# A deeper ring for raw weights in the first block, and four w_out parts split ahead

## The chip, the cores and the metric

The kernel runs on one core of a Trainium2 chip. The metric is the device time of one launch, in microseconds (us). Engines are named as in the profile: PE is TensorE's matrix multiply and PEld its weight load, DVE is VectorE, ACT is ScalarE, POOL is GpSimd, SP is SyncE, which here only issues transfers (SPq is its queue). L12 means line 12 of the kernel before.

## The reference

Attention in a window of 64 positions, then two layers of two matrix products each.

```python
def _attn_ref(q, k, v):            # (4, 8, 576, 64) each
    scores = scale * np.matmul(q, k.transpose(0, 1, 3, 2))
    ...
    mask = (rel >= 0) & (rel < 64)
    ...                            # softmax over the masked scores
    return np.matmul(attn, v)
def reference(...):
    x = attention, as (2304, 512)
    x = softplus(x @ w_in) @ w_out           # w_in (512, 2048), w_out (2048, 512)
    return piecewise_square(x @ w2_in) @ w2_out
```

softplus(h) is max(h, 0) + log1p(exp(-|h|)); the second layer's function is h for h >= 1, 0 for h <= -1 and (h + 1)^2 / 4 between.

## The kernel before, in words

**Split numbers.** Most products are taken with operands split into a high and a low part, both of the type fp32r: three matmuls (high by high, high by low, low by high) replace one of full f32.

**Weights.** Each layer's d_ff of 2048 is cut into 16 parts f. The host hands over the inputs viewed as 64-bit integers; a "raw" tile [128, 512, 2] of 512 KB holds one half of a part. Half j = 2f is the w_in part of f, half 2f + 1 its w_out part, for j below 32; the second layer's w_in has halves 32 to 47 and its w_out 48 to 63. `load_w` (L138) issues the next raw load from SP, into a ring of four tiles (`NRAW`, tag "raw"). The same ring also gives the tiles "o", in which `finish` (L428) collects a block's result before its store to x2d, and they come in the order of the program. Decoding a half is one ScalarE pass (`begin_half`, L162) and three VectorE passes (`end_half`, L167 to L169); when the opening is over, `end_half` of a first-layer half also calls `load_w`. `high` (L178, ScalarE) and `low` (L185, VectorE) make the two split parts. For w_in they go into the large tile `area`; for w_out (part 1) into tiles of the tags "wh1" (16 tiles of 2 KB per partition) and "wl1" (17).

**The first layer** goes over five blocks of tokens, 512, 256, 512, 512 and 512. For each block and part f, `g1` (L400) does 12 matmuls of x by w_in into one of two banks "h", `softplus` (L418, or L423 to L425 in the split form) makes g from it, and two steps later `g2` (L411) adds g by w_out into four banks "y". Block 0 differs: its w_out part is the decoded f32 tile `wo`, not split, and its g is one f32 tile, so that `g2` is a plain f32 product:

```python
if len(g) == 1:
    ops = [(wo[f][:, c], g[0])]
else:
    a, b = wh[0, f, 1], wl[0, f, 1]
    ops = [(a[:, c], g[0]), (a[:, c], g[1]), (b[:, c], g[0])]
```

From block 1 on everything is split. The loop over steps splits the parts `wo` into "wh1" and "wl1" tiles in block 1 (`osplit`), just ahead of their use. At the last step of block 1 it calls `load_w(3)` for the first three halves of the second layer; the steps of blocks 2 and 3 decode that layer's w_in (`decode_win`), and store it to DRAM (wd), and the last block splits its w_out (`split_wout`) into tiles of the same tags "wh1" and "wl1".

**Attention** for the next block runs between these steps: scores (L282), copies and mask (L304, L306, L310), maximum (L314, L315), exponentials (L319), normalising (L324 to L326), transposes (L336), masks (L346), values (L363), and x as high and low (L368, L371). Its q, k and v loads are issued from SP.

**The order of the work.** The opening, up to the first parts of block 0, is written out by hand in the list START: a letter for each operation (W a raw load, R and B the two stages of a decode, H and L high and low, G, U and Z the three stages of a part, S to Y the attention, K and J its loads). After it, and on engines that the list leaves idle, the framework's planner takes the ready instruction that comes first in the program, by its own estimate of times. So an instruction of a later block may run early: its place in the code is no more than its rank. Each engine then runs its list in this order, and waits where an input is late. Tiles of one tag are handed out in the order of the program.

Of the kernel before, what the change touches and what calls it, by code (L numbers as in the profile page):

```python
# [9 lines left out]
F32 = mybir.dt.float32  # L10
F32R = mybir.dt.float32r
I32 = mybir.dt.int32  # L12
# [5 lines left out]
NT, DM, DFF = B * S, H * D, 2048  # L18
P = 128
# [4 lines left out]
NF = DFF // P  # L24
# [15 lines left out]
HALF = 256  # L40
BEHIND = 8
NRAW = 4
NHALF = 4
NFIRST = 6


# [5 lines left out]
W5 A1 P0 B2 X0 E11 E10 H2 Y0 B3 N1 S2 C20 J1 C21 D20 W6 D21 T1 A2 E21 V10 V11 E20 P1 J2 N2 T2 L0 V21 V20 W7 P2  # L52
K3 J3 X1 R4 Y1 R5 X2 B4 H4 Y2 G00 L2 L4 U00 B5 S3 R6 W8 C30 C31 D30 D31 G20 R7 G10 J4 U20 Z20 A3 B6 B7 R8 E30
Z00 W9 E31 N3 T3 R9 U10 K4 Z10 H6 W10 L6 V30 R10 V31 G30 W11 B8 U30 P3 X3 W12 Z30 H8 R11 Y3 B9 B10 G11 U11 G31
H10 G01 L8 B11 U31 L10 W13 G21 Z11 U01 U21 G52 G42 Z01 U52 Z21 U42 Z31 Z52 Z42 J5
""".split()


# [1 line left out]
def tile_window_attention_two_ffn(  # L60
# [13 lines left out]
    wpool = ctx.enter_context(tc.tile_pool(name="weights", bufs=NF))  # L74
    spool = ctx.enter_context(tc.tile_pool(name="stage", bufs=3))
# [45 lines left out]
    def cut(at, n):  # L121
        return area[:, at:at + n]
# [9 lines left out]
    wh, wl, wo = {}, {}, {}  # L132
# [5 lines left out]
    def load_w(n=1, e=nc.sync):  # L138

        for _ in range(n):  # L140
            j = wnext[0]
            if j < (2 if wlimit[0] else 4) * NF:
                raw = spool.tile([P, DM, 2], I32, tag="raw", name="raw", bufs=NRAW)
                f, part = divmod(j, 2) if j < 2 * NF else (j % NF, j // NF - 2)
                e.dma_start(raw.rearrange("p c w -> p (c w)"),
                            (w1, w2)[j // (2 * NF)][f, :, 2 * DM * part:2 * DM * (part + 1)])
                raws[j] = raw
                wnext[0] += 1
# [3 lines left out]

    def begin_half(j):

        if j < 2 * NF and j % 2:
            t = wpool.tile([P, DM], F32, tag="wl1", name="wo", bufs=NF + 1)
            wo[j // 2] = t
            t = t.bitcast(I32)
        else:
            t = tpool.tile([P, DM], I32, tag="o", name="bits")  # L160
        decoded[j] = t
        A.activation(t.bitcast(F32), raws[j][:, :, 1].bitcast(F32), AF.Copy, scale=2.0 ** -112)  # L162

    def end_half(j):
        t, raw = decoded[j], raws.pop(j)
        lo, hi = raw[:, :, 0], raw[:, :, 1]
        V.tensor_scalar(t, t, 3, 1, op0=ALU.logical_shift_left, op1=ALU.bitwise_or)  # L167
        V.scalar_tensor_tensor(t, hi, -2 ** 31, t, op0=ALU.bitwise_and, op1=ALU.bitwise_or)  # L168
        V.scalar_tensor_tensor(t, lo, 29, t, op0=ALU.logical_shift_right, op1=ALU.bitwise_or)  # L169
        if not opening[0] and j < 2 * NF:  # L170
            load_w()

    def high(key, t, part):
        if part:
            wh[key + (part,)] = wpool.tile([P, DM], F32R, tag="wh1", name="wh1")
        else:
            wh[key + (part,)] = cut(2 * DM * key[1], DM)
        A.copy(wh[key + (part,)], t)  # L178

    def low(key, t, part):  # L180
        if part:
            wl[key + (part,)] = wpool.tile([P, DM], F32R, tag="wl1", name="wl1", bufs=NF + 1)
        else:
            wl[key + (part,)] = cut(2 * DM * key[1] + DM, DM)
        V.tensor_tensor(wl[key + (part,)], t, wh[key + (part,)].bitcast(F32), op=ALU.subtract)  # L185

    def split_w(f):
        for part in range(2):
            j = 2 * f + part
            begin_half(j)  # L190
            end_half(j)
            t = decoded.pop(j)
            if not part:
                high((0, f), t.bitcast(F32), 0)
                low((0, f), t.bitcast(F32), 0)

    kept = []

    def keep_w():

        while kept:
            f = kept.pop()
            nc.sync.dma_start(wd[f // 2][:, DM * (f % 2):DM * (f % 2 + 1)], decoded.pop(2 * NF + f).bitcast(F32))
            load_w()

    def decode_win(f):
        keep_w()
        begin_half(2 * NF + f)
        end_half(2 * NF + f)
        kept.append(f)  # L210
# [165 lines left out]
    def new_x():  # L376
        return [xpool.tile([P, KC, 512], F32R, tag=t, name=t) for t in ("xh", "xl")]

    def attn_items(block, xh, xl):

        t0, n = block
        items = []
        for i in range(n // P):
            a = attention(t0 // P + i, "a", "a", "a", xh, xl, i * P)
            items += [[(a["S"],), (a["C"], 0), (a["C"], 1), (a["D"], 0), (a["D"], 1), (a["A"],)],
                      [(a["E"], 0), (a["E"], 1), (a["N"],)],
                      [(a["T"],), (a["V"], 0), (a["V"], 1)],
                      [(a["P"],), (a["X"],), (a["Y"],)]]
        return items
# [24 lines left out]
    def softplus(h, n, split):  # L414

        if not split:
            g = gpool.tile([P, 512], F32, tag="gl", name="g")[:, :n]
            A.activation(g, h, AF.Softplus)  # L418
            return (g,)
        e = tpool.tile([P, 512], F32, tag="e", name="e")[:, :n]  # L420
        gh = gpool.tile([P, 512], F32R, tag="gh", name="gh")[:, :n]
        gl = gpool.tile([P, 512], F32R, tag="gl", name="gl")[:, :n]
        A.activation(gh, h, AF.Softplus)  # L423
        A.activation(e, h, AF.Softplus)  # L424
        V.tensor_tensor(gl, e, gh.bitcast(F32), op=ALU.subtract)  # L425
        return gh, gl

    def finish(block, y):  # L428
        t0, n = block
        per = 1024 // n  # L430
        for m0 in range(0, len(y), per):
            o = spool.tile([P, 1024], F32, tag="raw", name="o", bufs=NRAW)
            for m in range(m0, m0 + per):
# [52 lines left out]
    def load_x2(blk):  # L486

        for name, kc, hf in (("B11", 0, 0), ("B12", 0, 1), ("B22", 2, 1), ("B21", 2, 0)):
            if blk:
                st = spool.tile([P, 2, NW], F32, tag="raw", name="xs", bufs=NRAW)  # L490
            else:
# [12 lines left out]
    def split_x(name, slot):  # L504
        h, l = piece(slot)
        A.copy(h, xt[name])
        V.tensor_tensor(l, xt[name], h.bitcast(F32), op=ALU.subtract)
# [34 lines left out]
    def second(blk, p, g, t):  # L542
# [9 lines left out]
        if p == NQ - 1:  # L552
            o = spool.tile([P, DM], F32, tag="raw", name="o", bufs=NRAW)
            r = slice(WIDE * blk + t * P, WIDE * blk + (t + 1) * P)
# [9 lines left out]
    def emit(item, i, g):  # L564

        for step in item:
            step[0](*step[1:])
        d = g + i // 4 * 2
        if i % 4 < 2:
            load_qk(d + i % 4 + 2)  # L570
        elif i % 4 == 3:
            load_v(d + 4)
            load_v(d + 5)
# [5 lines left out]
    for i, (_, n) in enumerate(BLOCKS):  # L579
        kf = 512 // n  # L580
        steps += [(i, f, kf, 0, n) for f in range(0 if i else NFIRST, NF, kf)]
    pend = []
    wsplit = [0]
    osplit = [0]
# [57 lines left out]
    for i, f, kf, c0, n in steps:  # L642
        if i < last:
            nb = BLOCKS[i + 1][1] // P * 4
            if i + 1 not in xs:
                xs[i + 1] = new_x()
                queue = attn_items(BLOCKS[i + 1], *xs[i + 1])
            d = nb - len(queue)
            while d < ((f + kf) * nb // NF if i else (f + kf - BEHIND) * nb // (NF - BEHIND)):
                emit(queue.pop(0), d, BLOCKS[i + 1][0] // CB)  # L650
                d += 1

        if i == 0:
            while wsplit[0] < min(f + kf + AHEAD, NF):
                split_w(wsplit[0])
                wsplit[0] += 1
        if i == 1:
            while osplit[0] < min(f + kf, NF):
                t = wo.pop(osplit[0])
                high((0, osplit[0]), t, 1)  # L660
                low((0, osplit[0]), t, 1)
                osplit[0] += 1
            if f + kf == NF:
                wlimit[0] = False
                load_w(3)
        if 2 <= i <= 3 and f % 2:
            decode_win(NF // 2 * (i - 2) + f // 2)

        if i == last:
            if f == 0:  # L670
                keep_w()
                begin_second()
                load_x2(0)
                load_pair(0)
            if f == 3:
                combine(0)
                load_pair(1)
            if f >= 4:
                split_wout(f - 4)
            if f % 2 and f > 1:  # L680
                name = FIRST[f // 2 - 1]
                if name[0] == "T":
                    term(name)
                split_x(name, slots[name])
        h = pt("h")[:, :kf * n]
        for j in range(kf):
            g1(f + j, c0, n, *xs[i], h[:, j * n:(j + 1) * n])
        if len(pend) >= LAG:
            emit_g2(pend.pop(0))
        pend.append((i, f, kf, c0, n, softplus(h, kf * n, i > 0)))  # L690
    gfree = [[gpool.tile([P, 512], F32R, tag=t, name=t)[:, :NW] for t in ("gh", "gl")] for _ in range(3)]
    wide = [l1["pool"].tile([P, 2, NW], F32R, tag="g", name="g", bufs=4) for _ in range(3)]
    gfree += [[t[:, 0], t[:, 1]] for t in wide]
# [113 lines left out]
```

## Time and profile before

| | |
|---|---|
| median of 3 runs | 882.1 us (881.63 to 882.73) |
| the profiled execution | 879.26 us, of which the span from first to last instruction is 877.5 us |
| busy share PE, PEld, DVE, ACT | 96%, 82%, 66%, 47% |
| mean granted TensorE clock | 0.988 |
| raw weight loads | 64 of 512 KB, 4.9 us from issue to landing (median) |

The times of single instructions below come from that one profiled execution. Matmuls overlap, so the duration printed for one is longer than the step from its start to the next one's; a count of matmuls with the time of the whole run of them, as the chain gives it, is the better price.

### The profile page before, as it was taken

To read this page: it belongs to the slowest core of one execution; us is meant where nothing else is said; L and a number is where in the kernel's file an instruction comes from. 1 tells how busy PE (TensorE), PEld (TensorE's weight loads), DVE (VectorE), ACT (ScalarE), POOL (GpSimd) and SP (SyncE) were. 2 spreads that over 40 slices of the span, in tenths; PEclk is the share of its full clock that TensorE was granted. 3 is DMA by queue.
4 is the path that set the end of the run, shared out by engine and by line. 5 is a ranking of instruction groups with operands and counts; after the bars stand their busy time and mean duration, and the time that the engine had idled before them with its cause. 6 is when DMAs were issued, how large, how long until landed. Compare 5 with 4: busy or idle time off the path is not lost.

```text
span 877.5 us, 13083 instructions
## 1 busy us (share of the span) xinstructions
PE 846.5 (96%) x5032; PEld 715.5 (82%) x5032; DVE 578.1 (66%) x1101; ACT 411.6 (47%) x988; POOL 1.5 (0%) x10
## 2 busy tenths in 40 slices
PE   2699999999999999999999999999999999999998
PEld 2586666799888887888888889889899898998987
DVE  5998954654763356434766599768787668776753
ACT  4565622444442344333554465546545446454542
POOL 0000000000000000000000000000000000000000
PEclk9599999999999999999999999999999999999999
DMA  8676522643931166203532032010420101201001
GB/s 297 201 245 226 191 71 72 221 137 100 306 114 49 49 194 226 72 1 120 169 111 81 25 119 74 25 49 24 136 81 25 49 25 49 96 25 49 25 1 72
DMA packets 51805, 92.19 MB, mean 105 GB/s; under 512 B 5536, under 2 KB 25248, under 8 KB 51744
## 3 DMA queue, kind: packets, MB, share of 16 engines
q1 hardware_dynamic: 49216, 86.78, 30.0%
q10 hardware_dynamic: 2528, 4.59, 1.5%
q8 instruction: 39, 0.64, 0.3%
q14 instruction: 22, 0.18, 0.1%
HBM read 77.73 MB, written 13.63 MB: 104 GB/s over the span
## 4 chain that ended last, share of the span: by engine, by line
PE 88%; DMA 5%; DVE 4%; ACT 2%; issue 1%; SPq 1%; ACTq 0%
PE h L400 20%; PE y L411 20%; PE h L536 20%; PE y L551 15%; PE a L551 8%; DMA raw<-in_w 3%; PE a L363 2%; PE a L282 1%; DMA first<-in_q 1%; PE a L336 1%; ACT p L319 1%; DVE pt L346 1%; DMA wd<-bits 0%; DVE bits L168 0%; ACT bits L162 0%
## 5 line engine op out<-in xcount | busy, mean ns | idle before, releaser
L400 PE MATMUL h<-xh,area 128*128 128x512 f32 (+1 forms) x672 | 202.6, 371 | 1.5 <-ACT g L418 1.5
L536 PE MATMUL h<-area,ah 128*128 128x384 f32 x672 | 171.5, 336 | 0.0
L400 PEld LDWEIGHTS h<-xh,area 128*128 128x128 f32 x672 | 121.9, 190 | 24.1 <-issue 2.7
L536 PEld LDWEIGHTS h<-area,ah 128*128 128x128 f32 x672 | 123.2, 188 | 8.1 <-DVE c L527 0.2
L400 PE MATMUL h<-xl,area 128*128 128x512 f32 (+1 forms) x336 | 121.7, 362 | 0.0
L536 PE MATMUL h<-area,al 128*128 128x384 f32 x336 | 112.9, 336 | 0.0
L515 ACT ACTIVATE e<-e 128x384 f32<-128x384 f32 x96 | 50.0, 523 | 91.9 <-DVE e L514 91.9
L411 PE MATMUL y<-gl,wh 128*128 128x512 f32 (+1 forms) x256 | 92.9, 363 | 0.0
L411 PE MATMUL y<-gh,wl 128*128 128x512 f32 (+1 forms) x256 | 92.8, 363 | 0.0
L411 PE MATMUL y<-gh,wh 128*128 128x512 f32 (+1 forms) x256 | 92.8, 362 | 0.0
L551 PE MATMUL y<-wh,g 128*128 128x512 f32 x244 | 88.5, 393 | 0.0
L425 DVE TENSOR_TENSOR gl<-e,gh 128x512 fp32r<-128x512 f32 x56 | 38.6, 690 | 56.5 <-ACT e L424 56.2
L400 PEld LDWEIGHTS h<-xl,area 128*128 128x128 f32 x336 | 64.0, 191 | 9.4 <-issue 0.7
L423 ACT ACTIVATE gh<-h 128x512 fp32r<-128x512 f32 x56 | 33.3, 595 | 68.9 <-PE h L400 68.8
L536 PEld LDWEIGHTS h<-area,al 128*128 128x128 f32 x336 | 63.0, 188 | 0.0
L516 DVE TENSOR_TENSOR e<-c,e 128x384 f32<-128x384 f32 x96 | 53.1, 555 | 13.5 <-ACT e L515 12.5
L319 ACT ACTIVATE p<-p,mx 128x64 f32<-128x64 f32 x144 | 48.1, 339 | 22.8 <-DVE mx L315 22.8
L411 PE MATMUL y<-g,wo 128*128 128x512 f32 (+1 forms) x160 | 57.5, 507 | 0.0
L527 DVE TENSOR_TENSOR c<-h,m 128x384 f32<-128x384 f32 x48 | 26.6, 554 | 46.9 <-PE h L536 46.2
L411 PEld LDWEIGHTS y<-gl,wh 128*128 128x128 f32 x256 | 48.3, 189 | 7.6
L411 PEld LDWEIGHTS y<-gh,wh 128*128 128x128 f32 x256 | 48.3, 189 | 7.5
L411 PEld LDWEIGHTS y<-gh,wl 128*128 128x128 f32 x256 | 48.3, 189 | 7.5
(116 smaller groups left out, 1379.3 us busy)
## 6 DMA issues: line engine op xcount, KB each, us to landing
raw<-in_w SPq DMA_DIRECT2D x64, 512.0 KB, 4.9
ab<-wd SPq DMA_DIRECT2D x24, 512.0 KB, 3.3
qt<-in_q SPq DMA_DIRECT2D x34, 256.0 KB, 4.5
vt<-in_v SPq DMA_DIRECT2D x32, 256.0 KB, 3.1
kt<-in_k SPq DMA_DIRECT2D x29, 256.0 KB, 4.6
xs<-x2d SPq DMA_DIRECT2D x12, 384.0 KB, 4.5
wd<-bits SPq DMA_DIRECT2D x16, 256.0 KB, 4.1
x2d<-o SPq DMA_DIRECT2D x5, 512.0 KB, 3.1
```

What stands on the lines that cost most here:

```text
L282: T.matmul(banks[u][o, a2, s, lo:], qt[r, a, r], kt[r, a, -(2 * CB - lo):], start=True, stop=True)
L319: A.activation(k["sel"][:, i, :], k["sel"][:, i, :], AF.Softplus, bias=k["mx"][:, i:i + 1], scale=SCALE, accum_out=k["sm"][:, i:i + 1])
L363: T.matmul(k["po"][hf * CB:(hf + 1) * CB, a, s, :], vts[s][r, hd:hd + D], k["pt"][s][r, 2 * hf + a // 2, a % 2, :], start=True, stop=True)
L400: T.matmul(h, w, x, start=i == 0, stop=i == len(ops) - 1)
L411: T.matmul(y[m][:, c0:c0 + n], w, x, start=begin and i == 0, stop=f == NF - 1 and i == len(ops) - 1)
L423: A.activation(gh, h, AF.Softplus)
L425: V.tensor_tensor(gl, e, gh.bitcast(F32), op=ALU.subtract)
L515: A.activation(e, e, AF.Square, bias=0.5, scale=0.5)
L516: V.tensor_tensor(e, c, e, op=ALU.max)
L527: V.tensor_tensor(c, bank, other, op=ALU.add)
L536: T.matmul(bank, l[:, c], r[:, kc], start=begin and kc == i == 0, stop=kc == 1 and i == 2, skip_group_check=True)
L551: T.matmul(yw[t], l, r, start=p == j == i == 0, stop=p == NQ - 1 and j == 1 and i == 2)
```

## The change

Odd halves from 13 on (`FIRST_WIDE`) of the first layer are loaded into tiles of the tag "wh1", which now has 8 tiles of twice the size, each for the high parts of two neighbouring f. The list START gets four more loads, W14 to W17. The w_out halves of f = 12 to 15 (`SPLIT`) are decoded into the tile "bits" and split at once, and block 0 uses them split, with g split as well. Block 1 splits the other twelve. `load_w(3)` for the second layer stands at f = 8 of block 1, not at its last step.

```diff
-H10 G01 L8 B11 U31 L10 W13 G21 Z11 U01 U21 G52 G42 Z01 U52 Z21 U42 Z31 Z52 Z42 J5
+H10 G01 L8 B11 U31 L10 W13 G21 Z11 U01 U21 G52 W14 G42 Z01 U52 Z21 U42 Z31 Z52 W15 Z42 J5 W16 W17
...
+                if FIRST_WIDE <= j < 2 * NF and j % 2:
+                    raw = wpool.tile([P, DM, 2], I32, tag="wh1", name="raw", bufs=NF // 2)
+                else:
+                    raw = spool.tile([P, DM, 2], I32, tag="raw", name="raw", bufs=NRAW)
...
-        if j < 2 * NF and j % 2:
+        if j < 2 * SPLIT and j % 2:
             t = wpool.tile([P, DM], F32, tag="wl1", name="wo", bufs=NF + 1)
...
     def high(key, t, part):
         if part:
-            wh[key + (part,)] = wpool.tile([P, DM], F32R, tag="wh1", name="wh1")
+            if key[1] % 2 == 0:
+                highs[key[0]] = wpool.tile([P, 2, DM], F32R, tag="wh1", name="wh1", bufs=NF // 2)
+            wh[key + (part,)] = highs[key[0]][:, key[1] % 2]
...
-            if not part:
-                high((0, f), t.bitcast(F32), 0)
-                low((0, f), t.bitcast(F32), 0)
+            if not part or f >= SPLIT:
+                high((0, f), t.bitcast(F32), part)
+                low((0, f), t.bitcast(F32), part)
...
-            while osplit[0] < min(f + kf, NF):
+            while osplit[0] < min(f + kf, SPLIT):
...
-            if f + kf == NF:
+            if f == NF // 2:
                 wlimit[0] = False
                 load_w(3)
...
-        pend.append((i, f, kf, c0, n, softplus(h, kf * n, i > 0)))
+        pend.append((i, f, kf, c0, n, softplus(h, kf * n, i > 0 or f >= SPLIT)))
```

## Rows read from the trace of the kernel before

**Rows 1.** The page, part 1: busy time, share and instructions of each engine.
```profile
PE 846.5 (96%) x5032; PEld 715.5 (82%) x5032; DVE 578.1 (66%) x1101; ACT 411.6 (47%) x988; POOL 1.5 (0%) x10
```

**Rows 2.** Waits of PE: line, waited for; us in total, times, longest.
```profile
PE a L336 <- DVE p L326: 2.7, 3, 2.1
PE h L400 <- ACT g L418: 1.5, 1, 1.5
```

**Rows 3.** Busy by stretch: PE, PEld, DVE, ACT, POOL; granted clock, DMA share, GB/s.
```profile
0.00:40.00 40.00, 17.22 (x216) 14.06 (x216) 29.18 (x60) 19.16 (x69) 1.53 (x10) 0.76 0.76 254
...
110.00:144.00 34.00, 34.00 (x194) 20.95 (x196) 15.37 (x26) 7.21 (x25) 0.00 (x0) 1.00 0.19 61
...
200.00:300.00 100.00, 100.00 (x722) 82.97 (x722) 50.63 (x94) 38.64 (x118) 0.00 (x0) 1.00 0.40 129
```

**Rows 4.** The chain of waits, 72 to 95 us: start, length, what.
```profile
72.22 5.32 DMA raw<-in_w
...
80.98 0.70 DVE bits L169
81.68 0.02 SPq L145
...
81.73 4.87 DMA raw<-in_w
...
86.68 0.66 ACT bits L162
...
87.85 0.50 ACT g L418
...
91.45 3.43 PE y L411 x8
```

**Rows 5.** The chain in block 3, a part with split weights.
```profile
346.68 2.72 PE y L411 x12
```

**Rows 6.** Groups by line, 40 to 160 us: count, busy, mean ns, idle before.
```profile
L425 DVE TENSOR_TENSOR gl<-e,gh 128x512 fp32r<-128x512 f32 x2 | 1.4, 683 | 0.0
...
L424 ACT ACTIVATE e<-h 128x512 f32<-128x512 f32 x2 | 1.2, 584 | 0.0
```

**Rows 7.** The chain of waits, 158 to 170 us.
```profile
158.38 0.38 SPq L437
...
158.81 5.67 DMA raw<-in_w
...
165.09 2.75 ACT p L319 x16
...
169.15 0.63 PE a L336 x4
```

**Rows 8.** Timelines of ACT, DVE and PE, an attention step in block 0.
```profile
92.88 0.43 ACT L304 COPY p<-a 128x128 f32<-128x128 f32 x2
...
99.78 0.69 DVE L326 TENSOR_TENSOR p<-p,sm 128x512 f32<-128x512 f32 x1
...
100.89 0.60 PE L336 MATMUL a<-ident,p 128*128 128x128 f32 x4
```

**Rows 9.** Line 178 to 200 us: ns least, median, most; first and last start.
```profile
L178 ACT CAST wh<-wo x16: 601/620/638, 18.3 to 109.2; 128x512 fp32r<-128x512 f32 x16
```

**Rows 10.** Timelines of DVE, SP and ACT, 162 to 172 us.
```profile
162.49 0.17 DVE L315 TENSOR_SCALAR mx<-mx 128x8 f32<-128x8 f32 x1
...
163.43 1.82 SPq L145 DMA_DIRECT2D raw<-in_w  x2
...
170.97 0.68 ACT L162 ACTIVATE bits<-raw 128x512 f32<-128x512 f32 x1 [2.17 <-DMA raw<-in_w]
```

**Rows 11.** Busy by stretch, as rows 3: block 0, and a busy stretch for comparison.
```profile
60.00:100.00 40.00, 38.48 (x178) 27.14 (x177) 35.48 (x69) 25.90 (x60) 0.00 (x0) 1.00 0.77 268
...
320.00:340.00 20.00, 20.00 (x142) 16.11 (x141) 12.30 (x23) 7.55 (x18) 0.00 (x0) 1.00 0.96 327
```

**Rows 12.** Waits of ACT over the whole span, as rows 2.
```profile
ACT bits L162 <- DMA raw<-in_w: 20.1, 11, 3.3
```

More of the change, by code (lines that the diff above doesn't have):

```diff
@@ L42 @@
 NRAW = 4
+FIRST_WIDE = 12
 NHALF = 4
+SPLIT = 12
 NFIRST = 6
@@ L142, in load_w @@
             if j < (2 if wlimit[0] else 4) * NF:
-                raw = spool.tile([P, DM, 2], I32, tag="raw", name="raw", bufs=NRAW)
+                if FIRST_WIDE <= j < 2 * NF and j % 2:
+                    raw = wpool.tile([P, DM, 2], I32, tag="wh1", name="raw", bufs=NF // 2)
+                else:
+                    raw = spool.tile([P, DM, 2], I32, tag="raw", name="raw", bufs=NRAW)
                 f, part = divmod(j, 2) if j < 2 * NF else (j % NF, j // NF - 2)
@@ L171, in end_half @@
             load_w()
+    highs = {}
     def high(key, t, part):
         if part:
-            wh[key + (part,)] = wpool.tile([P, DM], F32R, tag="wh1", name="wh1")
+            if key[1] % 2 == 0:
+                highs[key[0]] = wpool.tile([P, 2, DM], F32R, tag="wh1", name="wh1", bufs=NF // 2)
+            wh[key + (part,)] = highs[key[0]][:, key[1] % 2]
         else:
```

## The prediction

> **What bounds the kernel now.** I read the page's first two parts, the waits of TensorE, the chain of waits with the timelines around TensorE's gaps, and last SP's and the DMAs' rows. TensorE is busy 846.5 of 877.5 us [rows 1]. Of the idle 31 us, 22.8 lie before 40 us (17.22 busy of 40), before anything that the diff edits takes effect; from 200 to 300 us there is none [rows 3]. So a change here has two ways to gain: fewer matmul microseconds, or TensorE's late gaps. Two of these are large: 1.5 us where block 0's first-layer matmul L400 waits for softplus L418, near 88 us, and 2.1 us, the longest of the three behind "DVE p L326", in block 1 [rows 2]. The latter I place at 169.15, where the chain ends in the transposes L336 [rows 7].
>
> The first gap, by the chain [rows 4]: VectorE ends the third decoding step of a half at 81.68, SP issues the next raw load 0.02 us later, it takes 4.87 us, and the decode's first step on ScalarE (L162) starts at 86.68. The softplus that frees the h bank stands behind it in ScalarE's queue and starts at 87.85. The load did not wait for the DMA engines: it waited for one of the four raw rooms.
>
> **The change part by part.**
>
> *f = 12 to 15 of block 0 take w_out split.* A part against plain f32 weights is 8 matmuls in 3.43 us [rows 4]; a part against split weights is 12 in 2.72 us, at the same width of 512 [rows 5]. Saved on TensorE: 4 x (3.43 - 2.72) = 2.84 us. TensorE has no gap from 110 to 144, where most of these parts lie (34.00 of 34.00 busy) [rows 3], so this comes off the end as long as nothing else becomes late. What it adds: four more softplus passes on ScalarE (584 ns) and four subtractions on VectorE (683 ns) [rows 6], 2.3 and 2.7 us, in a stretch where ScalarE is busy 7.21 and VectorE 15.37 of 34 us [rows 3]: nothing. Without that cover they would cost at most their sum, 5.0 us. The h bank is freed by two ScalarE passes instead of one, 0.6 us later; the blocks after, which always do this, show no gap from 200 to 300 us [rows 3]. The casts and subtractions for these four parts are moved, not added.
>
> *Raw halves in w_out's high room, W14 to W17, six halves ahead.* The odd halves from 13 on get eight rooms, so the ring of four serves the even ones alone: a room comes back after about eight halves instead of four. The loads on the chain stand one ring apart, at 72.22 and 81.73 [rows 4], so by estimate four halves, 9.5 us, of extra lead; some 2 us suffice for the gap to go. On SP four issues come forward into the opening; two v loads of block 1 stand behind two of them, under 1 us, and the values of block 1's second pair, which read them, run 70 us later: nothing. The first gap, 1.52 us, can then be worth between 1.52 gained and, since more transfers in flight may also land later, as much lost. I take 1.52 gained, since the chain names the room and not the transfer.
>
> What is late next there: the transposes at 100.89 start 0.4 us after VectorE's p L326 ends (99.78 + 0.69), and that chain began with ScalarE's copy at 92.88, 6 us after its scores, queued behind decode work [rows 8]. If TensorE arrives 1.5 us sooner and this chain does not move, 1.1 us comes back. It should move: the queue that held the copy is the one that stood waiting for raws before 86.68.
>
> *The high room is taken.* Before, the high casts for w_out of block 1 slip into ScalarE's queue from 18.3 us on [rows 9]. Now the twelve that are left can get room only as the last raws are decoded, so 12 casts of 0.62 us and 12 subtractions like those of [rows 6], 0.68 us, fall where VectorE and ScalarE have 18 and 26 us idle (110 to 144). Block 1 reads them at 163 us: cost nothing, and the opening loses casts. Pairing the high parts makes the second layer's first cast of a pair wait one part longer for its room; the stretch up to layer two has no TensorE gap, so I put nothing.
>
> *load_w(3) at f = 8 instead of 14.* In the trace the three loads are not at f = 14: the first is issued at 158.81, right behind the store of block 0's result, and the other two at 163.43, after four k and q loads [rows 7, 10]. The first cannot come before that result's rooms, which precede it in the ring, so it stays. The other two can pass the k and q loads, about 4 us sooner; those lose under 2 us and are read at 176.5.
>
> Around the second gap: the maximum that the exponentials wait for is ready at 162.66, but ScalarE stands before L162 until that raw lands and starts the exponentials at 165.09, 2.4 us late; the transposes wait 2.12 us [rows 2, 7, 10]. The store hangs on half of block 0's last part, the scores on all of it: that part's second half shrinks from 1.72 to 1.36 us, so the scores gain 0.36 us on the load and the gap grows to 2.5. Bounds: gone (2.12 gained, if the decode is queued behind the exponentials) to 6.6 us worse (below). I take +0.36, the order of before.
>
> **Sum.** -2.84 - 1.52 + 0.36 = -4.0 us. The profiled execution took 879.26 us with a span of 877.5, so 875.3 for it; it lies 2.8 below the median of the runs, 882.1, and the forecast is for that median: 878.1 us.
>
> **The rivals.**
>
> A, the forecast: 878.1.
>
> B: the decode of the first second-layer raw is queued behind the exponentials, both gaps go: -2.84 - 1.52 - 2.12 = -6.5, 875.6. For it: the 0.36 us by which the scores gain on the load may flip the order. Against: the load and the copies around it keep their order.
>
> C: with two loads issued side by side, the second half's decode also gets ahead of the exponentials. Before, it started at 170.97 [rows 10]; with its load 4.1 us sooner, 166.9, plus 0.68 for itself: exponentials at 167.5 instead of 165.09, 2.4 us. -4.36 + 2.4 = -2.0, 880.1.
>
> D, the other side: as C, but the second raw lands no sooner than now, because the stores and k and q loads around it fill the DMA engines. Exponentials at 170.97 + 0.68 = 171.65, 6.6 us late: -4.36 + 6.6 = +2.2, 884.3. It decides from where the exponentials start 4.36 us later than now, measured from the same scores. For it: that raw took 7.5 us to land before. Against: two decodes must stand ahead, where before it was one.
>
> E: the raws are asked for sooner and land no sooner, or the transposes' chain gives it back: the first gap stays, -2.84 + 0.36 = -2.5, 879.6. In 60 to 100 us the DMAs move 268 GB/s at a share of 0.77; another stretch reaches 327 at 0.96 [rows 11]. So there are 20% to spare, and eight waiting raws will use them up, but the halves need no more than a 2 us lead. The Trainium skill, "DMA: Bandwidth & Descriptors" (Issuing engines are not separate DMA queues), says that all transfers run on the same 16 engines and interleave, so asking early buys only what the engines have free; by that rule alone E would be the forecast. Here the trace speaks against the rule deciding: the share is 0.77, and the chain's load was issued 0.02 us after its room came free.
>
> That the third part does nothing it says is inside A: the first load stays where it is.
>
> **Chances.** A 0.37, B 0.20, E 0.13, C 0.17, D 0.13. A change of 0.2% (1.8 us) is about what can be told from none. A, B and E are faster (0.70), C ends at the bound: 0.05 faster, 0.12 same; D slower. Faster 0.75, same 0.12, slower 0.13. The range runs from below B, 875.0, to 882.0, past C; it leaves out D and little else.
>
> **What would show it.** Right: 12 matmuls in 2.72 us for block 0's last four parts; no wait behind "ACT g L418" near 87; ScalarE's waits for raws in L162, 20.1 us in all [rows 12], down to half or less; the casts "wh<-wo" starting near 100 us, not 18; the first second-layer raw right behind the x2d store, about 4 us earlier than 158.81. Wrong: a new TensorE gap in 60 to 110 (E), or a wait for p L326 in block 1 above 4 us (C, D), or below 1 (B). The whole forecast fails if TensorE shows new idle time past 200 us, where I put none.

## The result, and the profile after

The changed kernel takes 871.81 us (median of 4 runs, 870.92 to 872.67); the kernel before, timed beside it, 882.41 us (4 runs, 881.63 to 884.70). The ratio is 0.9898, with a 95% interval of 0.9877 to 0.992. The forecast was 878.1 us and the range ended at 875.0: the direction was right, the size was not.

The experiments below took 68 more runs of the kernel before; their median is 880.2 us, and so is that of all 72. The changed kernel, with four more runs (e8), has 872.0 us over eight. What has to be explained is therefore 8.2 us. The other 2.4 us of the first comparison lie in which runs it had.

The profiled executions took 870.92 us (span 869.2) after and 879.26 us (span 877.5) before. Here is part 1 of the page of the kernel after, with busy time, share and instructions of each engine.

```profile
PE 843.9 (97%) x5048; PEld 718.9 (83%) x5048; DVE 578.4 (67%) x1105; ACT 412.0 (47%) x992; POOL 1.5 (0%) x10
```

TensorE issues 16 more matmuls than in [rows 1], four parts with 12 in place of 8, and is busy 2.6 us less. VectorE and ScalarE each have the four instructions more that the diff adds. So busy time holds 2.6 of the 8.3 us by which the profiled executions differ, and the larger part was idle time. The waits of TensorE, after (line, waited for; us in total, times, longest), three of its groups:

```profile
PE a L345 <- ACT area L187: 0.6, 1, 0.6
...
PE y L560 <- DVE g L528: 0.2, 1, 0.2
...
PE a L345 <- DVE p L335: 0.2, 1, 0.2
```

Lines have moved by nine from `high` on (L335 is the L326 of [rows 2], L409 its L400) and by five ahead of it (L167 was L162). Both waits of [rows 2] that the prediction built on are gone. The wait for softplus has no row at all, as foreseen. The wait for p has shrunk from 2.7 us, with a longest of 2.1 in block 1, to a single one of 0.2 far behind, at 334.67; the forecast for the longest was 2.5. The stretches of [rows 3] and [rows 11] (PE, PEld, DVE, ACT, POOL; granted clock, DMA share, GB/s), after:

```profile
0.00:40.00 40.00, 19.47 (x248) 15.73 (x248) 30.19 (x62) 19.07 (x69) 1.52 (x10) 1.00 0.78 260
...
60.00:100.00 40.00, 40.00 (x180) 27.92 (x180) 37.70 (x73) 24.06 (x55) 0.00 (x0) 1.00 0.70 262
...
60.00:80.00 20.00, 20.00 (x76) 14.20 (x76) 19.08 (x37) 11.20 (x19) 0.00 (x0) 1.00 0.99 376
...
96.00:110.00 14.00, 14.00 (x77) 8.91 (x76) 13.44 (x23) 11.80 (x23) 0.00 (x0) 1.00 0.14 39
...
110.00:144.00 34.00, 34.00 (x225) 24.49 (x225) 16.23 (x29) 11.21 (x44) 0.00 (x0) 1.00 0.24 73
...
158.00:170.00 12.00, 12.00 (x143) 11.29 (x143) 9.99 (x20) 5.85 (x19) 0.00 (x0) 1.00 0.66 241
...
200.00:300.00 100.00, 100.00 (x683) 82.13 (x682) 49.59 (x93) 38.42 (x118) 0.00 (x0) 1.00 0.41 130
```

From 60 to 100 us TensorE has no gap left, where [rows 11] show 1.52 us of it. The mean DMA share of these 40 us, 0.70 for 0.77, hides what happened: in the first half it is 0.99 (376 GB/s), where the kernel before had 0.76 (264), and in the second half 0.42. So the raws that wait in more rooms did use up what the DMA engines had free, as rival E said, but the loads were over sooner and the gap went; E's time is out. The moved casts lie at 99.4 to 108.2 us (their row is below), not between 110 and 144 where the prediction put them, and TensorE has no gap there either (96 to 110). From 110 to 144 ScalarE has 4.0 us more to do, softplus passes and exponentials, and TensorE still no gap. From 200 to 300 us nothing new is late.

The chain of waits, after (start, length, what), where the first gap was, then in one of the four parts, then in block 1:

```profile
85.30 2.95 PE h L409 x12
...
88.25 3.43 PE y L420 x8
...
128.90 2.72 PE y L420 x12
...
154.19 3.07 PE h L409 x24
157.26 2.88 PE y L420 x24
160.14 0.84 PE h L409 x7
160.98 0.44 PE a L345 x4
```

In place of decode, load and softplus [rows 4] the chain holds TensorE alone. A part against split weights takes 12 matmuls in 2.72 us, as forecast. In block 1 the chain of [rows 7], from store to raw load to exponentials to transposes, is no longer there: TensorE goes from its own second-layer matmuls into the transposes.

What replaced it is seen on SP, which issues the loads of k, q and raws and the store of the first half of block 0's result in one order. SP's timeline after, 150 to 158 us:

```profile
150.68 0.37 SPq L150 DMA_DIRECT2D raw<-in_w  x1
...
152.82 0.39 SPq L446 DMA_DIRECT2D x2d<-o  x1
...
157.45 1.67 SPq L150 DMA_DIRECT2D raw<-in_w  x2
```

Before, the store went out at 158.38 and the first raw of the second layer right behind it, at 158.81 [rows 7]. Now that raw is asked for 2.14 us ahead of the store. The other two raws still stand behind the k and q loads. ScalarE and VectorE, after, at the same place:

```profile
154.78 0.70 ACT L167 ACTIVATE bits<-raw 128x512 f32<-128x512 f32 x1
...
156.40 0.16 DVE L324 TENSOR_SCALAR mx<-mx 128x8 f32<-128x8 f32 x1
...
156.66 0.35 ACT L328 ACTIVATE p<-p,mx 128x64 f32<-128x64 f32 x1 [1.19 <-DVE mx L324]
```

The raw has landed and its first decoding step (L167) is over at 155.48, 0.9 us before the last step on the maximum (L324) that the exponentials (L328) need. Before, this step stood ahead of them until 165.09 for a maximum ready at 162.66 [rows 7, 10]. Now the exponentials follow the maximum by 0.1 us, and ScalarE's last wait before them names the maximum and not the raw.

Two rows on the rest. The line that casts w_out's high parts (ns least, median, most; first and last start), and ScalarE's waits for raws (as [rows 12]):

```profile
L187 ACT CAST wh<-wo x12: 601/613/618, 99.4 to 108.2; 128x512 fp32r<-128x512 f32 x12
```

```profile
ACT bits L167 <- DMA raw<-in_w: 11.6, 7, 2.3
```

The casts start at 99.4 us in place of 18.3 [rows 9]. The waits for raws fall from 20.1 to 11.6 us [rows 12], not quite the half that the prediction named as its sign. In block 0 (40 to 110 us) they fall from 10.4 to 3.1 us, and that is the ring's doing: e1 below keeps the ring and has 3.5 there, e3 has the old ring and 9.8.

To see where the time went, the starts of the transposes L336 (L345 after) on TensorE in seven profiled executions, with the span. They come in groups of four matmuls, counted from T0; T3 ends the opening, and T7 is where the second gap was.

| kernel | T3 | T4 | T5 | T6 | T7 | T8 | T17 | span |
|---|---|---|---|---|---|---|---|---|
| before | 48.79 | 100.89 | 129.07 | 150.71 | 169.15 | 184.03 | 393.03 | 877.5 |
| after | 47.23 | 97.69 | 125.54 | 145.73 | 160.82 | 175.34 | 384.40 | 869.2 |
| after again (e8) | 48.07 | 98.53 | 126.38 | 146.58 | 161.66 | 176.18 | 385.47 | 870.3 |
| e1, no split | 48.38 | 98.84 | 126.70 | 148.33 | 166.92 | 183.17 | 392.53 | 877.5 |
| e9, no split, loads at f = 0 | 48.02 | 98.48 | 126.33 | 147.97 | 164.12 | 178.88 | 388.55 | 872.8 |
| e14, only f = 15 split | 49.69 | 100.21 | 128.06 | 149.70 | 168.25 | 184.12 | 393.72 | 878.4 |
| e15, split from f = 6 | 47.62 | 96.64 | 121.67 | 141.88 | 156.96 | 171.48 | 380.15 | 864.9 |

From before to after, stretch by stretch: T3 to T4 is 1.64 us shorter (the first gap), T4 to T5 0.33, T5 to T6 1.45 (two split parts, 2 x 0.71 = 1.42), T6 to T7 3.35 (the other two, and the second gap), T7 to T8 0.36; after T8 the two run alike within 0.4 us. These make 7.1 us. The opening makes 1.56 more, but 1.04 of that is there at 14 us, in matmuls that wait for the first q load, which the diff doesn't touch. The other 0.52 may belong to the granted clock, whose mean up to 40 us is 0.76 in the profile of before [rows 3] and 1.00 here. The row of those matmuls in TensorE's timeline, before:

```profile
14.16 1.98 PE L282 MATMUL y<-first 64*64 64x128 f32 x32 [7.16 <-DMA first<-in_q]
```

and after:

```profile
13.12 1.99 PE L291 MATMUL y<-first 64*64 64x128 f32 x32 [6.38 <-DMA first<-in_q]
```

The changed kernel's second profile (e8) has T3 at 48.07, so 0.84 of the 1.56 us can be the run and not the kernel.

### The profile page after: what moved, and what is told of

The parts are those of the page before. It is cut to its first block, busy times and chain, and to the rows that moved or that the text cites. A ratio compares the mean times of both kernels' runs of the same rounds, so it can differ in the third digit from the quotient of the medians.

```text
span 869.2 us, 13124 instructions
## 1 busy us (share of the span) xinstructions
PE 843.9 (97%) x5048; PEld 718.9 (83%) x5048; DVE 578.4 (67%) x1105; ACT 412.0 (47%) x992; POOL 1.5 (0%) x10
## 4 chain that ended last, share of the span: by engine, by line
PE 89%; DVE 4%; DMA 3%; ACT 2%; issue 1%; SPq 0%; ACTq 0%; DVEq 0%
PE h L409 22%; PE y L420 22%; PE h L545 19%; PE y L560 15%; PE a L560 7%; PE a L372 2%; PE a L291 1%; DMA first<-in_q 1%; PE a L345 1%; DMA raw<-in_w 1%; ACT p L328 1%; DMA ab<-wd 1%; DMA wd<-bits 1%; DVE pt L355 1%; DVE p L319 0%
## 5 line engine op out<-in xcount | busy, mean ns | idle before, releaser
L409 PE MATMUL h<-xh,area 128*128 128x512 f32 (+1 forms) x672 | 201.8, 370 | 0.0
L409 PEld LDWEIGHTS h<-xh,area 128*128 128x128 f32 x672 | 121.6, 190 | 22.5 <-issue 2.7
L409 PE MATMUL h<-xl,area 128*128 128x512 f32 (+1 forms) x336 | 121.9, 363 | 0.0
L420 PE MATMUL y<-gh,wh 128*128 128x512 f32 (+1 forms) x272 | 99.3, 365 | 0.0
L420 PE MATMUL y<-gl,wh 128*128 128x512 f32 (+1 forms) x272 | 99.2, 365 | 0.0
L420 PE MATMUL y<-gh,wl 128*128 128x512 f32 (+1 forms) x272 | 99.2, 365 | 0.0
L434 DVE TENSOR_TENSOR gl<-e,gh 128x512 fp32r<-128x512 f32 x60 | 41.4, 690 | 73.8 <-ACT e L433 73.6
L432 ACT ACTIVATE gh<-h 128x512 fp32r<-128x512 f32 x60 | 35.7, 594 | 89.3 <-PE h L409 89.3
L409 PEld LDWEIGHTS h<-xl,area 128*128 128x128 f32 x336 | 63.9, 190 | 9.4 <-issue 0.7
L328 ACT ACTIVATE p<-p,mx 128x64 f32<-128x64 f32 x144 | 48.1, 339 | 26.2 <-DVE mx L324 26.2
L420 PEld LDWEIGHTS y<-gh,wh 128*128 128x128 f32 x272 | 51.3, 189 | 8.2
L536 DVE TENSOR_TENSOR c<-h,m 128x384 f32<-128x384 f32 x48 | 26.6, 554 | 47.4 <-PE h L545 47.2
L420 PEld LDWEIGHTS y<-gh,wl 128*128 128x128 f32 x272 | 51.3, 189 | 8.1
L420 PEld LDWEIGHTS y<-gl,wh 128*128 128x128 f32 x272 | 51.4, 189 | 8.0
L560 PEld LDWEIGHTS y<-wh,g 128*128 128x128 f32 x244 | 45.8, 188 | 8.5 <-DVE g L528 0.7
```

The lines of the kernel that those rows point to most:

```text
L328: A.activation(k["sel"][:, i, :], k["sel"][:, i, :], AF.Softplus, bias=k["mx"][:, i:i + 1], scale=SCALE, accum_out=k["sm"][:, i:i + 1])
L409: T.matmul(h, w, x, start=i == 0, stop=i == len(ops) - 1)
L420: T.matmul(y[m][:, c0:c0 + n], w, x, start=begin and i == 0, stop=f == NF - 1 and i == len(ops) - 1)
L536: V.tensor_tensor(c, bank, other, op=ALU.add)
L560: T.matmul(yw[t], l, r, start=p == j == i == 0, stop=p == NQ - 1 and j == 1 and i == 2)
```

## The experiments

Two questions. What is each part worth? And why did the second gap go: because the second layer's loads are asked for at f = 8, because of the wider ring, or because of the split? Unless said otherwise an edit is to the kernel after. Times are medians with range and number of runs, ratios are to the kernel before in the same rounds, with 95% intervals.

**e1: no split.**

```diff
-SPLIT = 12
+SPLIT = 16
```

> The changed kernel with SPLIT = 16: all sixteen w_out parts of block 0 stay f32, the deeper ring and the early second-layer loads remain. Theory 1, the parts add up: 2.84 us above the changed kernel (871.8), so about 874.6, with 8 matmuls in 3.43 us in block 0's last four parts and no other difference. Rival: the split also shortens the path into block 1 (the result of block 0 is ready sooner), so its loss brings back part of the 2.1 us wait for p in block 1: 875.5 to 877.

Measured: 878.84 us (876.82 to 880.27, 11 runs), ratio 0.9978 [0.9966, 0.999]. The split is worth 6.8 us, far more than its 2.84 us of matmuls and more than either theory allowed. SP and TensorE in e1, timelines:

```profile
156.00 0.39 SPq L446 DMA_DIRECT2D x2d<-o  x1
156.43 0.47 SPq L150 DMA_DIRECT2D raw<-in_w  x1
```

```profile
166.92 1.09 PE L345 MATMUL a<-ident,p 128*128 128x128 f32 x4 [2.27 <-DVE p L335]
```

Without the split the raw is back behind the store, in the order of [rows 7], and the wait for p is back with 2.27 us. The wider ring and the loads at f = 8 are both still there, so neither of them removes the second gap by itself. What they do without the split, 880.2 - 878.8 = 1.4 us, fits the first gap: from T3 to T4 e1 takes the 50.46 us of the kernel after, where before took 52.10.

**e2: the loads late again.**

```diff
-            if f == NF // 2:
+            if f + kf == NF:
```

> The changed kernel with load_w(3) back at the last step of block 1. Theory 1: the early loads are what took away the wait for p in block 1, because the first second-layer raw now goes out ahead of the store of block 0's result: the wait comes back with 2.1 to 2.5 us, 873.9 to 874.3. Rival: the deeper ring emptied the four raw rooms sooner and this alone lets that load go ahead of the store: 871.8, and the raw is still issued before the store.

Measured: 872.96 us (872.32 to 873.10, 4 runs), 0.9911 [0.9893, 0.993]; the interval overlaps that of the change. The raw still goes out ahead of the store:

```profile
151.65 0.37 SPq L150 DMA_DIRECT2D raw<-in_w  x1
...
153.79 0.39 SPq L446 DMA_DIRECT2D x2d<-o  x1
```

Asking for the loads at f = 8 did nothing here that can be told from the spread of the runs.

**e3: the old ring.**

```diff
-FIRST_WIDE = 12
+FIRST_WIDE = 32
...
-H10 G01 L8 B11 U31 L10 W13 G21 Z11 U01 U21 G52 W14 G42 Z01 U52 Z21 U42 Z31 Z52 W15 Z42 J5 W16 W17
+H10 G01 L8 B11 U31 L10 W13 G21 Z11 U01 U21 G52 G42 Z01 U52 Z21 U42 Z31 Z52 Z42 J5
```

> The changed kernel with all raw halves in the ring of four and without W14 to W17; split and early loads remain. Theory 1: only the wait for softplus in block 0 comes back, 1.5 us: 873.3. Rival: the ring is also what took the high casts out of the opening and with that kept the opening short (1.6 us by the two profiles, and some 2 us more between medians than between profiles): 875 to 877, and high casts wh<-wo again from about 18 us on.

Measured: 873.18 us (871.76 to 873.98, 5 runs), 0.9914 [0.9894, 0.9934]. A wait for softplus is there again, 0.5 us; TensorE's timeline:

```profile
85.94 0.50 PE L409 MATMUL h<-xh,area 128*128 128x512 f32 x1 [0.52 <-ACT g L427]
```

It is shorter than the 1.5 us of before, though the ring is the same, and from T3 to T4 e3 takes 0.73 us longer than the kernel after; so with the split in place the ring is worth less than the whole first gap. The raw is ahead of the store here too (151.52 and 153.66), so the ring is not what turned that order. With the casts back in the opening the transposes T3 start at 47.35, no later than with the wide ring: taking them out of the opening gained nothing there.

**e4: the loads at f = 8, alone in the kernel before.**

```diff
-            if f + kf == NF:
+            if f == NF // 2:
```

> The kernel before with load_w(3) moved to f = 8 and nothing else. Theory 1: 2.1 us gained, 880.3, the wait for p in block 1 gone and the first second-layer raw issued ahead of the store. Rival, as the prediction had it: the first load stays behind the store, 882.4, the wait for p at 2.1 us or more.

Measured: 880.51 us (878.42 to 882.09, 12 runs), 0.9996 [0.9983, 1.0008]: no effect. The store is issued at 159.50 and the raw at 159.93, and the waits of TensorE are those of before:

```profile
PE a L336 <- DVE p L326: 3.7, 4, 2.3
...
PE h L400 <- ACT g L418: 1.6, 1, 1.6
```

**e5: half of the split.**

```diff
-SPLIT = 12
+SPLIT = 14
```

> The changed kernel with SPLIT = 14, so that only the last two parts of block 0 are split. Theory 1: the split of the parts that end block 0 is what lets the first second-layer load go ahead of the store; the wait for p in block 1 stays away, and only 2 x 0.71 = 1.4 us of TensorE time come back: 873.2, and no run shows the lower granted clock of about 0.998. Rival: the order turns on the whole shift of 2.84 us; the wait of 2.1 us is there, and 877.4 with the lower clock in half of the runs.

Measured: 873.86 us (872.79 to 876.37, 6 runs), 0.9931 [0.9914, 0.9948]. The two parts given up cost 1.9 us, by the matmuls 1.42. The raw is issued at 153.06, ahead of the store at 155.20, and the transposes in block 1 wait for nothing. Two split parts, f = 14 and 15, are enough.

**e6: one of the loads at f = 0, without the split.** It was to bring the raw forward in another way.

```diff
-SPLIT = 12
+SPLIT = 16
...
-            if f == NF // 2:
+            if f == 0:
                 wlimit[0] = False
-                load_w(3)
+                load_w(1)
+            if f == NF // 2:
+                load_w(2)
```

> The changed kernel without the split (SPLIT = 16, 878.8), and the first second-layer raw requested at the first step of block 1, ahead of block 0's result in the ring and on SP. Theory 1: the wait for p and the clock falls that follow it hang on the place of this one load: the wait goes (2.1 us, and about 1 us more on average for the clock), 875.7, and no run at 0.998. Rival: the split removes the wait by itself, by moving the exponentials: 878 to 879 and the wait of 2 us stays.

Measured: 876.13 us (875.44 to 878.21, 6 runs), 0.9955 [0.994, 0.997]. The first raw did go out at 88.15, but the second took its old place, at 155.65 right behind the store at 155.23, and a wait for p of 1.9 us stayed. So this run doesn't tell what the place is worth; e9 does.

**e7: split from f = 8.**

```diff
-SPLIT = 12
+SPLIT = 8
```

> The changed kernel with SPLIT = 8: eight parts of block 0 split. If each split part is worth 3.43 - 2.72 = 0.71 us of TensorE time and nothing becomes late: 2.84 us below the changed kernel, 869.0. Rival: VectorE, over 90% busy up to 110 us, cannot take four more subtractions (2.7 us) ahead of their use, and TensorE waits in block 0: 870.5 to 873.

Measured: 870.81 us (870.03 to 873.08, 5 runs), 0.9899 [0.9881, 0.9917]. Of 4 x 0.71 = 2.8 us, 1.2 arrive. A wait far behind the edit, 0.23 us in the kernel after (at 334.67), has grown to 1.60; TensorE's timeline:

```profile
334.38 0.63 PE L345 MATMUL a<-ident,p 128*128 128x128 f32 x4 [1.60 <-DVE p L335]
```

**e8: the kernel after, again.** No edit.

> The changed kernel once more, beside the kernel before in the same rounds: 871.8 plus or minus 1, no run with the granted clock at 0.998 or 0.986, only 1.0 or 0.988 (a fall in the opening), and the opening's transposes between 47 and 49 us, since the opening varies with the landing of the first q load and not with the change. Rival: the opening is shorter by 1.6 us because of the change: transposes at 47.2 again.

Measured: 872.28 us (871.28 to 873.14, 4 runs), 0.9908 [0.9891, 0.9925]. The opening came out 0.84 us longer than in the first profile, and no other stretch of the table differs by over 0.3.

**e9: all three loads at f = 0, without the split.**

```diff
-SPLIT = 12
+SPLIT = 16
...
-            if f == NF // 2:
+            if f == 0:
```

> The changed kernel without the split (SPLIT = 16, 878.8), and load_w(3) at the first step of block 1: all three second-layer raws go out before block 0 ends, so that no decode waits for a load next to the store of its result. Theory 1: the wait for p in block 1 comes from the place of these loads, not from the speed of the parts: it goes, 2.1 to 2.5 us, and with it the clock falls (0.998, about 1 us on average): 875 to 876, and the stretch from block 0's last transposes to those after them shortens from 18.6 to about 16.5 us. Rival: the split alone does it: 878 to 879, 18.6 us.

Measured: 874.34 us (873.49 to 876.19, 6 runs), 0.9942 [0.9928, 0.9956], 4.5 us less than e1 (3.2 by the ratios, which take out the drift between rounds). SP and TensorE in e9:

```profile
88.56 6.07 SPq L150 DMA_DIRECT2D raw<-in_w  x3
...
155.63 0.38 SPq L446 DMA_DIRECT2D x2d<-o  x1
```

```profile
164.12 0.60 PE L345 MATMUL a<-ident,p 128*128 128x128 f32 x4
```

All three are issued between 88.56 and 94.63, over 60 us before the store, the transposes wait for nothing, and T6 to T7 takes 16.15 us in place of e1's 18.59: 2.44 us, with not one matmul changed. So the place of these loads, and not the pace of the matmuls, is the cause of the second gap. None of 6 runs of e9 shows the slower clock that 6 of 11 of e1 show (last section); the wait of 2.3 us and 6 of 11 x 1.7 = 0.9 us for the clock make up the 3.2.

**e10: f = 12 to 14 split, f = 15 not.** The edit replaces the number by a tuple, where the last part keeps w_out's plain f32; by an oversight f = 15's high part lands in f = 11's room, so that f = 11 is taken with a wrong high part from then on. e13 has the same work with rooms of its own, and its times are the ones to go by.

```diff
-SPLIT = 12
+SPLIT = (12, 13, 14)
...
-        if j < 2 * SPLIT and j % 2:
+        if j < 2 * NF and j % 2 and j // 2 not in SPLIT:
...
-            if not part or f >= SPLIT:
+            if not part or f in SPLIT:
...
-        pend.append((i, f, kf, c0, n, softplus(h, kf * n, i > 0 or f >= SPLIT)))
+        pend.append((i, f, kf, c0, n, softplus(h, kf * n, i > 0 or f in SPLIT)))
```

> The changed kernel with only f = 12, 13 and 14 of block 0 split; the last part, f = 15, stays f32. Theory 1: what puts the first second-layer load ahead of the store is the pace of the part that ends block 0 (its four banks finish 0.68 us apart when split, 0.86 when not): here the store is first again, the wait of 2.1 us is back and about every second run shows the clock at 0.998: 871.9 + 0.7 + 2.1 + 1 = 875.7. Rival: it is the total shift of the block (2.1 of 2.8 us is still there): 872.6, no wait.

Measured: 877.08 us (875.80 to 879.40, 9 runs), 0.9975 [0.9963, 0.9987]. The store (153.03) is ahead of the raw (153.46) again, and the longest wait for p is 3.0 us.

**e11: only the split.** Old ring (both lines of e3), late loads (e2).

```diff
-FIRST_WIDE = 12
+FIRST_WIDE = 32
...
-            if f == NF // 2:
+            if f + kf == NF:
```

> The changed kernel with the old ring of four, the old START and load_w(3) at the last step: the split of four parts is all that is left. Theory 1: it carries 2.84 us of matmuls, the 2.1 us wait and the clock falls behind it, and lacks only the wait for softplus in block 0 (1.5 us): 873.2, as with the early loads. Rival: the early loads matter where the ring is old: 874.5 to 875.5.

Measured: 873.01 us (872.30 to 875.39, 6 runs), 0.9929 [0.9916, 0.9942]. Alone the split brings 7.2 of the 8.2 us (880.2 - 873.0). The raw (153.73) is ahead of the store (155.86), and the wait for softplus is 1.0 us.

**e12: split from f = 8, loads at f = 0.**

```diff
-SPLIT = 12
+SPLIT = 8
...
-            if f == NF // 2:
+            if f == 0:
```

> The changed kernel with SPLIT = 8 and load_w(3) at the first step of block 1, tried as a better version. SPLIT = 8 alone gained 2.1 us up to block 2 and lost 1.1 us of it at a wait for p near 335 us, where a decode waits for a load behind the store of block 2's result. Theory 1: three loads taken earlier shift the later loads too and that wait shrinks: 869.5 to 870.5. Rival: the loads behind block 2's store keep their place: 870.8.

Measured: 871.93 us (871.53 to 873.24, 5 runs), 0.9914 [0.9902, 0.9926]; no better than e7. TensorE waits 3.7 us for p in four places, 1.63 of it at 125.08 (0.57 in e7) and 1.28 at 335.22 (1.60 in e7): with the order already turned, asking still sooner is worth nothing.

**e13: e10 with rooms of its own.** As e10, and

```diff
-            if key[1] % 2 == 0:
-                highs[key[0]] = wpool.tile([P, 2, DM], F32R, tag="wh1", name="wh1", bufs=NF // 2)
-            wh[key + (part,)] = highs[key[0]][:, key[1] % 2]
+            pair = key[0], key[1] // 2
+            if pair not in highs:
+                highs[pair] = wpool.tile([P, 2, DM], F32R, tag="wh1", name="wh1", bufs=NF // 2)
+            wh[key + (part,)] = highs[pair][:, key[1] % 2]
```

> As the run with f = 12, 13 and 14 split and f = 15 left f32, but with each high part in its own room (there, f = 15's high part fell into f = 11's room). The store of block 0's result stands ahead of the first second-layer load on SP. Theory 1, the place of this load makes the wait: wait for p in block 1 of 2.1 to 3.0 us, clock at 0.998 or 0.986 in about two of three runs, 877. Rival, the earlier run's slowness had to do with its shared room: 872.6.

Measured: 877.66 us (876.80 to 878.67, 10 runs), 0.9977 [0.9965, 0.9988]. TensorE's timeline (lines one further on):

```profile
164.69 0.63 PE L346 MATMUL a<-ident,p 128*128 128x128 f32 x4 [2.48 <-DVE p L336]
```

Three of the four parts are split, which saves their 2.1 us of matmuls, and yet the time is 5.7 us above the change's: without the last part the raw stays behind the store (153.91 and 153.49) and the wait stays.

**e14: only f = 15 split.** As e13, with

```diff
-SPLIT = 12
+SPLIT = (15,)
```

> Only the last part of block 0, f = 15, is split; on SP the store of the result again stands ahead of the first second-layer load. Theory 1, the place on SP decides and not the split itself: the wait stays and, since the scores gain 0.36 us on the load, as the prediction reckoned, is about 2.5 us: 878.8 - 0.7 + 0.4 = 878.5. Rival, a split last part takes the wait away whatever the place of the load: 875.5, no wait.

Measured: 878.55 us (876.53 to 880.14, 11 runs), 0.9979 [0.9968, 0.9991]. SP and TensorE:

```profile
156.84 0.39 SPq L447 DMA_DIRECT2D x2d<-o  x1
157.28 0.47 SPq L150 DMA_DIRECT2D raw<-in_w  x1
```

```profile
168.25 1.09 PE L346 MATMUL a<-ident,p 128*128 128x128 f32 x4 [2.75 <-DVE p L336]
```

Here the last part is shorter and the raw still behind the store, just as the prediction had it for the change. The wait is 2.75 us (forecast 2.5). That it grew by the last part's doing is not shown: with the last part unsplit the profiles have 2.12 (before), 2.27 (e1), 2.31 (e4), 2.48 (e13) and 3.00 us (e10). The last part alone does not turn the order either; e5's f = 14 and 15 together do.

**e15: split from f = 6.**

```diff
-SPLIT = 12
+SPLIT = 6
```

> SPLIT = 6, as a better version: all parts that block 0 takes after the opening are split. 6 x 0.71 = 4.3 us below the changed kernel if nothing is late: 867.7. By what SPLIT = 8 did (2.1 of 2.8 us up to block 2, then a new wait of 1.1 us near 335 us), rather 870 to 871, no better than SPLIT = 8.

Measured: 866.93 us (866.71 to 867.32, 4 runs), 0.985 [0.9837, 0.9864]: better than both kernels, 5.1 us below the change and below the expected 870 to 871. Its page, and its wait for p:

```profile
PE 839.8 (97%) x5072; PEld 723.4 (84%) x5072; DVE 583.2 (67%) x1111; ACT 415.6 (48%) x998; POOL 1.5 (0%) x10
```

```profile
PE a L345 <- DVE p L335: 0.5, 1, 0.5
```

TensorE is busy 4.1 us less than after. In the table T3 to T4 is 1.44 us shorter than after and T4 to T5 2.82, together 4.26 = 6 x 0.71, and nothing is given back later. The rest of the 5.1 lies in the runs. Why e7 pays a wait at 334 us and this kernel, split further, doesn't, stays open.

## Why the prediction was wrong, step by step

- *Bounds.* Right: matmul time and two gaps, and both gaps were where they were placed.
- *Split parts, -2.84.* Right: 12 matmuls in 2.72 us; T5 to T6, which has two of them and nothing else, is 1.45 us shorter for 1.42. But two of the four, not most, lie in the stretch from 110 to 144; before, f = 14 and 15 ran at 147.4 and 156.0, just ahead of the store and the second gap.
- *First gap, -1.52.* Right: 1.64 in the profiled pair. Without the split the ring brings 1.4 us (e1); with it 1.2 by the medians of e3, of which its profile shows 0.73 at T4.
- *What is late next, 1.1 us to lose at T4.* Right that it would move: T4 comes 1.64 us earlier, measured from T3.
- *High room, 0.* Right, though the casts run at 99.4 to 108.2 us and not in the idle time from 110 to 144: no gap at either place, and none from 200 to 300.
- *load_w(3) at f = 8, nothing on the path.* Right as to what that line does (e2, e4), though its second and third loads did not pass the k and q loads as foreseen (SP's timeline after).
- *Second gap, +0.36.* Wrong, and this is the step that failed: "The first cannot come before that result's rooms, which precede it in the ring, so it stays", and from it "the order of before". It was checked for the line that moves the loads and not for the split, with which the order on SP turned: the first raw is asked for 2.14 us ahead of the store and 8.1 us earlier than before, 3.15 of these when measured from T6. Standing behind the result's rooms in the ring does not bind the load to the store: `finish` takes two of the four rooms for its tiles "o", the first second-layer raw takes the next one, which a raw of block 0 had held, and the kernel after shows it going out first. In place of +0.36 stood -2.1 for the wait. Where the order does stay (e14) the wait stays too, 2.75 us for 2.5.
- *Rival B* had the wait go because the decode would fall behind the exponentials. The wait went, but the decode stayed in front of them, and its data were early; that its 875.6 came nearest was luck. B also lacked the next term. C and D had the second half's decode ahead of the exponentials too; it starts at 162.72 us, over 3 us behind the last of them.
- *A term that no case had.* A wait for p in block 1 is often followed by a stretch of slower clock (last section), worth 1.7 us where it comes.

The 8.2 us, before to after, are then: 2.84 of matmuls; 1.5 for the first gap; 2.1 for the second; 43 of 68 runs of before x 1.7 = 1.1 on average for the clock that went with it; and some 0.7 of small differences, T4 to T5 and T7 to T8. The range's end at 875.0 lay just below B's sum, without the clock and those, from a median of 882.1 that the longer series puts at 880.2.

Open: why two split parts at the end turn the order of SP's issues, and one doesn't. The runs show when it happens (f = 14 and 15 both split: after, e2, e3, e5, e7, e11, e15; not e1, e10, e13, e14). That the planner's costs make the store ready later against the raw when the last two parts are timed differently is an argument only; no run varied those costs.

## What to carry over

Where one queue issues both the loads and the stores, an edit that changes the pace of the work around them can change their order; before writing "it stays behind", work out the order for every part of the edit, not only for the one that names the load. And price a wait of the busiest engine together with what comes after it: here the microseconds behind it cost 1.7 us where they came, nearly as much as the wait. When a sum misses, an experiment that takes one part away (e1) finds the part in one run; the runs that give the suspected place without that part (e9), or most of that part without the place (e13), show the cause.

## What the runs showed of the hardware

TensorE's clock often falls after the wait for p in block 1. The windows of e1 (columns as in [rows 3]), around that wait at 164.65 to 166.92:

```profile
162.00:166.00 4.00, 2.64 (x23) 2.44 (x21) 2.14 (x5) 3.73 (x19) 0.00 (x0) 1.00 1.09 384
166.00:168.00 2.00, 1.08 (x5) 1.11 (x6) 1.34 (x3) 0.56 (x2) 0.00 (x0) 0.71 1.03 419
168.00:170.00 2.00, 2.00 (x12) 2.00 (x11) 1.91 (x3) 0.68 (x1) 0.00 (x0) 0.50 0.36 138
170.00:172.00 2.00, 2.00 (x27) 1.79 (x26) 1.96 (x5) 0.68 (x1) 0.00 (x0) 0.94 0.00 0
```

The granted clock is 1.00 up to the wait, falls with the transposes behind it to 0.50, the lower of its two levels (1.2 of 2.4 GHz), and is back within the last window. The fall lasts 3.4 us, so it costs 1.7 us of work. e10, e13 and e14 show the same fall in their profiles, of the same length. The profiles of before and of e4 have nearly the same wait, 2.12 and 2.31 us, and no fall: the granted clock stays at 1.00 behind it. For the other runs only the mean granted clock is known. A fall of 3.4 us to half takes 0.002 off it, so 0.995 to 0.998 is read as a run with the fall, and 0.986 as one that also had the slow stretch in the opening (0.988 in the profile of before, which has 0.52 from 20 to 40 us). By this reading it was 43 of 68 of the kernel before, with a mean of 880.76 us against 879.10 in the other 25, 1.67 us apart; 6 of 11 of e1, 8 of 12 of e4, 7 of 9 of e10, 7 of 10 of e13 and 11 of 11 of e14, all with a wait of 2.1 to 3.0 us there in their one profile. Of 49 runs of the kernels without that wait (after, e2, e3, e5, e7, e8, e9, e11, e12, e15) none had it, nor did any of 6 of e6, whose wait was 1.9 us. So such a wait is followed by the fall in some executions and not in others, 82 of 121, and what decides between them wasn't found.

The other surprise is the opening: with no change to the first q load, the transposes that end it (T3) start anywhere from 47.2 to 49.7 us over the profiles in the table, and the same kernel (after, e8) differs by 0.84. Gains of under a microsecond that lie ahead of T3 can't be read from one pair of profiles.
